# One core, attention then a SiLU block: stores moved to ScalarE's queue, early products regrouped, one bank turned, two sums of k moved

## The chip, the cores and the metric

The kernel runs on one core of one Trainium2 chip. The metric is the device time of one launch in microseconds, as the median of several runs. Engines are called PE (TensorE's matmuls), DVE (VectorE), ACT (ScalarE), POOL (GpSimd) and SP (SyncE); a "q" behind a name (SPq, ACTq) means the engine's instruction queue, from which it also issues DMAs.

## The reference, cut to what matters

```python
# q, k, v: (8 batches, 12 heads, 448 positions, 64), float32
rmsnorm = lambda x, g: x / sqrt(mean(x * x, -1) + 1e-6) * g
scores = (rmsnorm(q, g_q) @ rmsnorm(k, g_k).T) / 8
attn = softmax(scores, -1) @ v                  # (8, 12, 448, 64)
x = attn with heads side by side                # (3584, 768)
h = x @ w_in                                    # w_in (768, 2048)
out = (h * sigmoid(h)) @ w_out                  # w_out (2048, 768)
```

Everything is float32.

## The kernel before, in words

**Order of the work.** One program is written out by hand, engine by engine; each engine takes its instructions strictly in the order in which they were issued. Attention comes in 24 stretches `c`, each for four heads of one batch, so three stretches make a batch and six (`GROUP`) make two batches. A stretch is a `visit(c)` (line 1270) followed by a `between(c)` (line 1342). After stretch 5 the products with `w_in` for a finished pair of batches are laid between the stretches of the next pair; the products of the last pair, and all products with `w_out` (`quad`), come after stretch 23.

**A visit.** `scores` (L595) writes four score tiles into one of two PSUM buffers named `sc`; ACT takes their exponential (L600) and frees the buffer. There are seven such calls to a visit. `weigh` (L627) multiplies the exponentials with v into the PSUM tiles `av0` and `av1`. The visit also finishes the attention of the stretch before: for early stretches DVE copies `av` out (L1297), later ones are divided at once (`divide`, L685); `weigh(c, 0, 1)` can start only when `av` has been read.

**Beside a visit.** While stretch c runs, q and k of c+1 are normalised: `do((i, 0))` is a square on ACT (L402), `do((i, 1))` its sum on DVE (L403), a scale-and-shift (L427) and a power on POOL (L431); i = 0, 1 are the halves of q, 2, 3 those of k. For q, POOL then scales the rows (L446), and PE transposes them in `between` (L559). The flag `behind` chooses where `do((0, 1))` stands, before or after the copy of `av`. From stretch 6 on the same parts stand in the lists `further` of `between`.

**Between.** `between(c)` transposes q of c+1, calls `fill`, transposes k of c+1 (L577), adds up the exponentials (`sum_up`, L661), inverts the sums on DVE (L670, 1.5 us for each half) and spreads the reciprocals over the partitions by six SP DMAs (L677), and calls `fill` again. `fill` takes matmuls from a generator up to a due number of columns, and deals other pieces of work between them. One product is three steps, or six MATMUL instructions of 128x448.

**Products with w_in.** `Seven` makes 2x2 blocks by seven products (Strassen's way, Winograd's form). A product's PSUM bank comes from `bank`: during attention there are only the two banks `mm`, so product n+2 waits until the result of product n has been read, by ACT for the products named "1" and "5" (L781, L791), by DVE for the others (`plus`, L728), some of which POOL completes (L793, L794). After stretch 23 six more banks (`alone`) replace the attention's PSUM tiles, and every fourth product takes `mm`:

```python
        turn = turns["next"] = (turns["next"] + 1) % 4
        if ps_alone is None or turn == 0:
            return ps_mm.tile([P, BANK], F32, name="mm")[:, 0:n]
        return ps_alone.tile([P, BANK], F32, name="alone")[:, 0:n]
```

`make_ahead` computes two pairs of products of the first group in stretches 3 to 5 and stores them to DRAM (`ahead`); `fetch_ahead` brings them back. `begin` gives a generator to `fill`, with the columns due at each call. In stretches 0 to 5 `sum_up` also takes an `mm` bank.

**Stores.** When a block's two rows are complete, `activate` (line 909) takes SiLU of each on ACT (L911) and calls `save` (line 805), which stores the row to `hidden` in DRAM. The rows live in three buffers called `stage`, so a later block waits for these stores. In the last part `fetch` reads `hidden` back.

**SP's queue** carries nearly all DMAs, in order: q, k, v, the weights, the spreads, the stores of the rows and of the output. ACT's queue carries two tiny loads at the start and four small stores of the output at the very end.

**At the start** `keep_busy(4)` runs four idle 128x128 float32 matmuls, before and after a tiny transposition (L348) that needs the gains.

Of the kernel before, what the change touches and what calls it, by code (L numbers as in the profile page):

```python
# [180 lines left out]
def kernel(  # L181
# [25 lines left out]
    nc = tc.nc  # L207
# [50 lines left out]
    def load_v(c):  # L258
        main, _ = keys_of(v, c)
        dst = place["v"].rearrange("p (n j d) -> p n j d", n=4, j=z.KEYS - 1)  # L260
        nc.sync.dma_start(dst, main[:, :, 0 : z.KEYS - 1])
# [44 lines left out]
    with tc.manual_schedule(), tc.tile_pool(  # L306
        name="ps_first", bufs=1, space=bass.MemoryType.PSUM
    ) as ps_first:
        load_q(0, first_q, True, 2)
        load_k(0)  # L310
        load_q(1, second_q, True)
        load_v(0)
        for i, g in enumerate((g_q, g_k)):
            nc.scalar.dma_start(g1[:, i, :], g.rearrange("(one d) -> one d", one=1))
        load_k(1)
        load_v_rest(0)
        room.w_in.load()
        load_v_rest(1)
        nc.gpsimd.memset(minus_half, -0.5)
        make_identity(nc, ident)  # L320
        nc.scalar.activation(first, minus_half, AF.Square)


        nc.gpsimd.memset(ones[:, 0], 1.0)
        for i in range(2):
            for half in range(2):
                rows = ds(half * z.LEFT, z.LEFT)
                nc.gpsimd.memset(ones[rows, 1 + i], 1.0 if i == half else 0.0)

        wide = [g1[:, i : i + 1, :].to_broadcast([1, 2, D]) for i in range(2)]  # L330
        nc.vector.tensor_tensor(out=both, in0=wide[0], in1=wide[1], op=ALU.mult)
        nc.vector.tensor_reduce(
            out=most, in_=both[:, 0, :], axis=AX.X, op=ALU.max, apply_absolute_value=True
        )
        nc.vector.tensor_scalar(
            out=small, in0=most, scalar1=float(SCORE_MAX / D**0.5), scalar2=None, op0=ALU.is_le
        )


        idle = ps_first.tile([P, P], F32, name="idle")  # L340
        column = ps_first.tile([P, BANK], F32, name="column")[:, 0:1]

        def keep_busy(n):
            for _ in range(n):
                nc.tensor.matmul(idle, ident, ident, start=True, stop=True)

        keep_busy(4)
        nc.tensor.transpose(column, both.rearrange("p two d -> p (two d)"), ident[0:1, 0:1])  # L348
        nc.vector.tensor_scalar_mul(out=gains, in0=column, scalar1=float(D) ** -0.5)
        keep_busy(4)  # L350

        for i in range(2):
            norm.squares_q(0, first_q, first_squares[i], i)()
            norm.root(0, "q", i)
        for i in range(2):
            norm.squares_k(0, place["k0"], first_squares[i], i)()
            norm.root(0, "k", i)
            norm.scale(0, first_q, place["q0"], i, nc.vector)
# [105 lines left out]
def bounded(  # L464
# [3 lines left out]
    P, D, R, J, S = z.P, z.D, z.R, z.J, z.S  # L468
    HW, HF = z.NW // 2, z.NF // 2
# [8 lines left out]
    GROUP = z.NPAIR  # L478
# [3 lines left out]
    hidden = dram.tile([z.NF, P, z.B * S], F32, name="hidden")  # L482
# [60 lines left out]
    def x_of(c, i):  # L543
        b, cp = divmod(c, z.NPAIR // 2)
        return xT(b, 2 * cp + i)
# [205 lines left out]
    turns = dict(next=0)  # L751
# [49 lines left out]
    def staged():  # L801
        stages.append(stages.pop(0))
        return stages[-1]

    def save(f, column, t):
        nc.sync.dma_start(hidden[f, :, ds(column, t.shape[1])], t)


    AHEAD = 2
    ahead = dram.tile([AHEAD, P, 2 * S], F32, name="ahead")  # L810

    def make_ahead(group):
        for m in range(AHEAD):
            row = staged()
            yield from part_in(group, m, [row, row], True).two()
            nc.sync.dma_start(ahead[m], row)
# [384 lines left out]
    def begin(work, columns, parts):  # L1201
        finish()
        filler.update(work=work, due=0.0, share=columns / parts)
# [31 lines left out]
    def finish():  # L1235
        run(filler["work"])
# [33 lines left out]
    def visit(c):  # L1270

        beside = normalise(c + 1) if c <= GROUP else []

        def do(*which):

            if beside:
                for i, part in which:
                    beside[i][part]()

        behind = GROUP // 2 < c < GROUP  # L1280
        if c < NC:
            scores(c, 0, 0)
        do((0, 0))
        if not behind:
            do((0, 1))
        if c > 0:
            weigh(c - 1, LEFT)
            weigh(c - 1, LEFT - 1, 0)
        if c < NC:
            scores(c, 0, 1)  # L1290
        if c == 0:
            do((1, 0), (1, 1))
        if c > 0:
            weigh(c - 1, LEFT - 1, 1)
            if c - 1 < EARLY:
                for i in range(2):
                    nc.vector.tensor_copy(x_of(c - 1, i), sums[i])  # L1297
                if behind:
                    do((0, 1))
                do((1, 0), (1, 1))  # L1300
                if inverting:
                    if c > 1:
                        divide(c - 2, None)
                    run_all(inverting)
                    inverting.clear()
            else:
                divide(c - 1, sums)
                do((1, 0), (1, 1))
                if c < NC and c % GROUP == 0:
                    for i in summed_x(c):  # L1310
                        sum_x(last_two(c), i, range(3))
                if c == NC:
                    sum_x(last_two(c), 0)
                weights_in_visit(c)
            if c + 1 < NC:
                loads["vrest"](c + 1)
        if c == NC:
            return
        scores(c, 1, 0)
        scores(c, 1, 1)  # L1320
        if c < GROUP:
            do((2, 0))
        weigh(c, 0, 1)
        scores(c, 2, 0)
        if c < GROUP:
            do((3, 0))
        weigh(c, 1, 1)
        scores(c, 2, 1)
        weigh(c, 0, 0)
        run_all(add(c, 1))  # L1330
        if c < GROUP:
            do((2, 1), (3, 1))
        weigh(c, 1, 0)
        scores(c, LEFT)
        if c + 1 < NC:
            loads["v"](c + 1)

    def run_all(work):
        for piece in work:
            piece()  # L1340

    def between(c):

        def transposes_and_sums():
            summing = sum_up(c)
            if c < GROUP:
                next(summing)
            if c < NC - 1:
                transpose_k(c + 1)
            reciprocals = next(summing)  # L1350
            if GROUP // 2 <= c <= EARLY:
                divide(c - 1, None)
            return reciprocals

        if c < NC - 1:
            transpose_q(c + 1)
        if c < GROUP // 2:
            inverting.extend(transposes_and_sums())
        elif c == GROUP - 1:
            run_all(transposes_and_sums())  # L1360
        if c >= GROUP and c % GROUP == 0:
            fetched = range(AHEAD) if c == GROUP else ()
            columns = products - 2 * HW * S * len(fetched)
            work = halves_in(last_two(c), range(HF), plain_in, dict(begun), fetched)
            begin(work, columns, 2 * GROUP)
            begun.clear()
        late = add(c, LEFT - 1) + add(c, LEFT) if c >= GROUP else []
        further = [
            lambda a=a: run_all(a) for a in (normalise(c + 2) if c >= GROUP - 1 else [])
        ]  # L1370
        rest = []
        if c >= GROUP and c % GROUP == 0:
            rest = [lambda i=i: sum_x(last_two(c), i, (3,)) for i in summed_x(c)]
        fill(rest + late + weights_in(c, 0) + further[2:])
        prompt = transposes_and_sums() if GROUP // 2 <= c != GROUP - 1 else []
        if c == GROUP // 2:
            begin(make_ahead([0, 1]), AHEAD * 2 * HW * S, GROUP - 1)
        fill(weights_in(c, 1) + (further[:2] if c >= GROUP else []), prompt)
        if c % GROUP == GROUP - 1:
            finish()  # L1380
            if c == GROUP - 1:
                begun[0] = fetch_ahead([0, 1], 0)
            elif c < NC - 1:
                sum_x([c // GROUP * 2, c // GROUP * 2 + 1], 0)
        if GROUP <= c < NC - 1:

            nc.scalar.activation(first, minus_half, AF.Exp)
        if c == NC - 1:
            while rounder.load():
                pass  # L1390
# [12 lines left out]
    ps_alone = ctx.enter_context(  # L1403
        tc.tile_pool(name="ps_alone", bufs=6, space=bass.MemoryType.PSUM)
    )
    turns["next"] = 1
    group = [z.B - 2, z.B - 1]
    for i in (1, HW - 1):
        sum_x(group, i)
# [217 lines left out]
```

## Time and profile before

| | |
|---|---|
| three runs | 1351.76, 1352.02, 1356.16 us; median 1352.02 |
| the profiled run | 1354.68 us, its span 1352.8 us |
| busy, share of the span | PE 98%, DVE 68%, PEld (weight loads) 62%, ACT 38%, POOL 25% |
| stretches 0 to 5, to the first product of stretch 6 | 0 to 140 us |
| stretches 6 to 23 | 140 to 768 us |
| last pair's products with `w_in`, then those with `w_out` | 768 to 895 us, then to the end |
| `hidden` stores | 64 of 448 KB, issued by SP, median 2.7 us to landing |

Times are counted from the span's start. "Idle before" is the time in which an engine did nothing before an instruction, with what ended the wait behind the arrow; a chain of waits names, for each engine, who waited for whom and for how long in all, how often, and at most. In a row of the timeline the first number is the start, the second the length of a merged run of equal instructions.

### The profile page before, as it was taken

How to read it: one execution, taken by the hardware profiler on the slowest of the kernel's cores; microseconds unless marked ns; L12 is line 12 of the kernel's file. 1: busy time of each engine (PE TensorE's matmuls, PEld its weight loads, DVE VectorE, ACT ScalarE, POOL GpSimd, SP SyncE). 2: the span in 40 equal slices, each digit the busy share in tenths (PEclk: the TensorE clock that was granted, in tenths of full speed). 3: DMA queues.
4: the chain of work that ended last, by engine and by line, in shares of the span. 5: the costliest groups of instructions: out<-in, count | busy, mean ns of one | idle time of the engine just before them, and what ended most of it. 6: DMA issues, size and time to landing. Idle time of an engine off the chain costs nothing.

```text
span 1352.8 us, 19797 instructions
## 1 busy us (share of the span) xinstructions
PE 1323.9 (98%) x7345; PEld 837.8 (62%) x7345; DVE 921.2 (68%) x1593; ACT 517.4 (38%) x884; POOL 340.6 (25%) x241
## 2 busy tenths in 40 slices
PE   8999999999999999999999999999999999999997
PEld 4333444444444444444444455557999999999997
DVE  5887867785654444644443587679878787878785
ACT  7866565555455545454644244320000010101000
POOL 5655533343233332333221144420000000000001
PEclk9999999999999999999999999999999999999999
DMA  8554436323223223322321248521423232322311
GB/s 226 163 148 134 118 94 174 104 79 87 71 84 92 79 75 90 85 79 79 79 79 38 100 160 264 159 97 45 127 74 98 75 98 78 101 87 91 112 60 39
DMA packets 175422, 139.42 MB, mean 103 GB/s; under 512 B 104052, under 2 KB 159284, under 8 KB 175316
## 3 DMA queue, kind: packets, MB, share of 16 engines
q1 hardware_dynamic: 174640, 137.08, 34.3%
q8 instruction: 60, 0.98, 0.3%
q0 software_dynamic: 352, 0.79, 0.2%
q14 instruction: 46, 0.38, 0.1%
q10 hardware_dynamic: 324, 0.20, 0.1%
HBM read 88.47 MB, written 41.29 MB: 96 GB/s over the span
## 4 chain that ended last, share of the span: by engine, by line
PE 87%; DVE 5%; issue 3%; ACT 2%; DMA 1%; POOL 1%; SPq 0%; ACTq 0%; DVEq 0%; POOLq 0%
PE mm L773 28%; PE alone L1080 22%; PE av L627 8%; PE mm L1080 7%; PE sc L595 7%; PE alone L773 7%; PE alone L1117 2%; PE sc L559 1%; PE sc L577 1%; PE sc L661 1%; DVE work L670 1%; PE mm L1117 1%; ACT work L600 1%; PE mm L661 1%; DVE work L641 0%
## 5 line engine op out<-in xcount | busy, mean ns | idle before, releaser
L773 PE MATMUL mm<-x,W 128*128 128x448 f32 x636 | 255.4, 545 | 4.5 <-DVE stage L728 2.2
L600 ACT ACTIVATE work<-sc,rms 128x448 f32<-128x448 f32 x324 | 184.6, 633 | 91.1 <-PE sc L595 80.4
L431 POOL TENSOR_TENSOR rms<-rms,minus_half 128x14 f32<-128x14 f32 (+4 forms) x55 | 136.2, 2478 | 252.5 <-DVE rms L427 158.2
L773 PEld LDWEIGHTS mm<-x,W 128*128 128x128 f32 x636 | 118.4, 191 | 126.9 <-issue 107.3
L773 PE MATMUL mm<-sums_x,W 128*128 128x448 f32 x456 | 183.3, 542 | 1.4 <-DVE parts L728 1.1
L641 DVE TENSOR_TENSOR work<-work 128x896 f32<-128x896 f32 (+1 forms) x114 | 125.0, 1129 | 65.9 <-ACT work L600 65.4
L595 PE MATMUL sc<-work 64*64 64x448 f32 x1344 | 164.2, 547 | 1.7 <-ACT work L600 0.7
L627 PE MATMUL av<-work,rows 64*64 64x448 f32 x1296 | 152.5, 544 | 7.5 <-issue 2.6
L773 PEld LDWEIGHTS mm<-sums_x,W 128*128 128x128 f32 x456 | 85.1, 190 | 87.5 <-issue 80.6
L458 POOL DMA_DIRECT2D out_dram<-x x4 | 2.2, 565 | 442.7 <-DVE x L728 442.7
L627 PEld LDWEIGHTS av<-work,rows 64*64 64x64 f32 x1296 | 51.9, 132 | 94.6 <-issue 84.1
L595 PEld LDWEIGHTS sc<-work 64*64 64x64 f32 x1344 | 52.1, 133 | 83.7 <-issue 37.1
L1080 PE MATMUL alone<-W,rows 128*128 128x192 f32 x488 | 92.0, 326 | 0.0
L403 DVE TENSOR_REDUCE rms<-squares 112x8 f32<-112x512 f32 (+1 forms) x80 | 52.4, 655 | 55.1 <-ACT squares L402 54.3
L793 POOL TENSOR_TENSOR parts<-parts,stage 128x448 f32<-128x448 f32 x31 | 42.1, 1358 | 176.4 <-DVE parts L728 176.2
L1080 PEld LDWEIGHTS alone<-W,rows 128*128 128x128 f32 x488 | 81.4, 190 | 0.0
L1080 PE MATMUL alone<-W,work 128*128 128x192 f32 x382 | 72.2, 326 | 0.0
L911 ACT ACTIVATE stage<-stage 128x896 f32<-128x896 f32 x63 | 57.2, 945 | 26.0 <-DVE stage L728 25.4
L402 ACT ACTIVATE squares<-rows 128x512 f32<-128x512 f32 (+1 forms) x74 | 44.8, 605 | 50.6 <-DVE rms L403 49.3
L1080 PEld LDWEIGHTS alone<-W,work 128*128 128x128 f32 x382 | 63.8, 190 | 0.0
L1090 ACT COPY squares<-alone 128x192 f32<-128x192 f32 x34 | 10.8, 318 | 138.0 <-PE alone L1080 79.0
L685 DVE TENSOR_TENSOR x<-av,work 128x448 f32<-128x448 f32 x38 | 22.0, 620 | 60.9 <-PE av L627 60.5
(248 smaller groups left out, 2153.4 us busy)
## 6 DMA issues: line engine op xcount, KB each, us to landing
hidden<-stage SPq DMA_DIRECT2D x63, 448.0 KB, 2.7
work<-hidden SPq DMA_DIRECT2D x21, 1024.0 KB, 4.9
rows<-in_moe_w_out_dram SPq DMA_DIRECT2D x32, 384.0 KB, 3.5
W<-in_moe_w_in_dram SPq DMA_DIRECT2D x22, 512.0 KB, 4.8
rows<-in_k_dram SPq DMA_DIRECT2D x48, 192.0 KB, 3.1
work<-work SPq DMA_DIRECT2D x144, 56.0 KB, 1.9
rows<-in_q_dram SPq DMA_DIRECT2D x36, 224.0 KB, 3.5
x<-hidden SPq DMA_DIRECT2D x7, 1024.0 KB, 5.6
```

The costliest lines, as they stand in the source:

```text
L402: nc.scalar.activation(t, rows, AF.Square)
L403: return lambda: nc.vector.tensor_reduce(out=out, in_=t.rearrange("p (n d) -> p n d", n=n), axis=AX.X, op=ALU.add)
L431: nc.gpsimd.tensor_tensor(out=t, in0=t, in1=half, op=ALU.pow)
L595: nc.tensor.matmul(two[ds(half * D, D), h, 0:S], keys[rows, ts(half, D)], qT[rows, pair, :], start=True, stop=True,)
L600: nc.scalar.activation(eleft[:, h] if j == LEFT else weights(c, j)[:, i, h], two[:, h, 0:S], AF.Exp, scale=norm.column(c, i, h, j),)
L627: nc.tensor.matmul(sums[i][ds(h * D, D), :], v, w, start=(j == 0 and step == 1), stop=(j == LEFT - 1 and step == 1),)
L641: nc.vector.tensor_tensor(out=total, in0=total, in1=more, op=ALU.add)
L773: nc.tensor.matmul(t, self.left(name, s), self.right(name, s), start=s == ends[0], stop=s == ends[1])
L793: nc.gpsimd.tensor_tensor(out=u2, in0=u2, in1=p5, op=ALU.add)
L911: nc.scalar.activation(t, t, AF.Silu)
L1080: nc.tensor.matmul(t, x[:, i], y, start=i == ORDER[0], stop=i == ORDER[-1])
L1117: nc.tensor.matmul(o, a[:, 2 * i + m, t], right_one(name, i)[:, m], start=n == 0, stop=n == len(steps) - 1,)
```

## The change

It does five things:

- the stores of `save` are issued by ACT's queue instead of SP's;
- `begin` gives `make_ahead` its columns in 4 parts instead of 5: one whole product at each of four calls of `fill` (stretch 3's second, both of stretch 4, stretch 5's first), where before they were 3, 2, 3, 2 and 2 matmul steps;
- `turns["next"]` starts at 3 after attention, so the last group's first product takes a bank `mm`, and the following three take `alone`;
- `behind` now means stretches 1 to 3 instead of 4 and 5. In stretches 4 and 5 q's first sum moves ahead of the copy of `av`, and in stretches 0, 4 and 5 k's two sums follow their squares instead of standing at the end of the visit. In stretches 1 to 3 the order stays what it was;
- one more idle matmul at the start.

```diff
-        keep_busy(4)
+        keep_busy(5)
         nc.tensor.transpose(column, both.rearrange("p two d -> p (two d)"), ident[0:1, 0:1])
...
     def save(f, column, t):
-        nc.sync.dma_start(hidden[f, :, ds(column, t.shape[1])], t)
+        nc.scalar.dma_start(hidden[f, :, ds(column, t.shape[1])], t)
...
-        behind = GROUP // 2 < c < GROUP
+        behind = 0 < c <= GROUP // 2
         if c < NC:
             scores(c, 0, 0)
-        do((0, 0))
-        if not behind:
-            do((0, 1))
+        do((0, 0), (0, 1))
...
                     nc.vector.tensor_copy(x_of(c - 1, i), sums[i])
-                if behind:
-                    do((0, 1))
                 do((1, 0), (1, 1))
...
         if c < GROUP:
-            do((2, 0))
+            do((2, 0)) if behind else do((2, 0), (2, 1))
         weigh(c, 0, 1)
         scores(c, 2, 0)
         if c < GROUP:
-            do((3, 0))
+            do((3, 0)) if behind else do((3, 0), (3, 1))
...
-        if c < GROUP:
+        if behind:
             do((2, 1), (3, 1))
...
-            begin(make_ahead([0, 1]), AHEAD * 2 * HW * S, GROUP - 1)
+            begin(make_ahead([0, 1]), AHEAD * 2 * HW * S, AHEAD * 2)
...
-    turns["next"] = 1
+    turns["next"] = 3
```

## The prediction

> **What bounds the kernel.** First the engines' shares, then PE's waits:
>
> ```profile
> PE 1323.9 (98%) x7345; PEld 837.8 (62%) x7345; DVE 921.2 (68%) x1593; ACT 517.4 (38%) x884; POOL 340.6 (25%) x241
> ```
>
> ```profile
> PE mm L773 <- DVE stage L728: 2.4, 2, 2.2
> PE mm L773 <- DVE parts L728: 2.1, 2, 1.1
> PE alone L773 <- DVE x L685: 1.2, 1, 1.2
> PE av L627 <- DVE x L1297: 1.0, 2, 0.8
> ```
>
> PE is the bound; only its waits (some 22 us in all) can be gained, and any new one is lost in full. I then placed these waits. The longest is in stretch 4 (timeline, DVE's row, then PE's):
>
> ```profile
> 100.00 1.54 DVE L670 RECIPROCAL work<-mm 128x224 f32<-128x224 f32 x1
> 101.46 0.56 DVE L728 TENSOR_TENSOR stage<-mm,stage 128x448 f32<-128x448 f32 x1
> ```
>
> ```profile
> 102.07 3.30 PE L773 MATMUL mm<-x,W 128*128 128x448 f32 x4 [2.20 <-DVE stage L728]
> ```
>
> A product begun in one fill ends in the next, so its reading stands behind a reciprocal, and the next product has no bank. The four matmuls after it take 3.30 us, not 4 x 0.376. The stage table says why (length, PE, PEld, DVE, ACT, POOL busy, then PEclk):
>
> ```profile
> 98.40:101.70 3.30, 1.47 (x10) 0.30 (x2) 3.30 (x4) 1.07 (x2) 1.19 (x1) 1.00 0.30 65
> 101.80:105.10 3.30, 3.03 (x4) 1.17 (x4) 3.23 (x6) 0.00 (x0) 1.43 (x1) 0.50 0.99 287
> ```
>
> The clock fell to 0.50 for one stretch: 1.6 us lost.
>
> Then ACT, DVE and PE beside the saves. Stretch 11 (ACT's rows, then DVE's):
>
> ```profile
> 323.76 1.79 ACT L911 ACTIVATE stage<-stage 128x896 f32<-128x896 f32 x2
> 325.45 0.62 ACT L402 ACTIVATE squares<-rows 128x512 f32<-128x512 f32 x1
> 326.82 0.52 ACT L402 ACTIVATE squares<-rows 128x384 f32<-128x384 f32 x1 [0.75 <-DVE rms L403]
> ```
>
> ```profile
> 326.10 0.69 DVE L403 TENSOR_REDUCE rms<-squares 128x8 f32<-128x512 f32 x1 [3.36 <-ACT squares L402]
> 326.70 0.61 DVE L728 TENSOR_TENSOR stage<-mm,stage 128x448 f32<-128x448 f32 x1
> 328.05 1.55 DVE L670 RECIPROCAL work<-sc 128x224 f32<-128x224 f32 x1
> 329.52 0.56 DVE L728 TENSOR_TENSOR parts<-mm,stage 128x448 f32<-128x448 f32 x1
> ```
>
> The SiLUs end, k's squares follow with no gap, DVE idles for them, and behind its sums stand two readings of banks. The second ends at 330.08; PE takes that bank at 330.33: 0.25 us of slack. What ACT does longer before 325.45, PE pays but for 0.25.
>
> Last, what an issue on ACT's queue costs (the kernel's end):
>
> ```profile
> 1343.03 0.55 ACTq L458 DMA_DIRECT2D out_dram<-work  x1
> 1343.67 0.32 ACT L1094 COPY rows<-alone 128x192 f32<-128x192 f32 x1 [5.20 <-PE alone L1080]
> ```
>
> The copy's product ended at 1343.27; the copy before it (1338.15) began 0.08 us after its product, this one 0.40 after, 0.10 behind the issue. The issue seems to hold ACT.
>
> **The Trainium skill.** "TensorE: Matmul & The Clock Gate", section "Architectural detail", says that ACT and DVE are strict FIFO: the rows above agree. The same page, "What's actually happening", gives a free-running window of 3413 ns after whose activity the clock is set; the half-speed stretch of about 3.4 us fits. "DMA: Bandwidth & Descriptors", section "Issuing engines are not separate DMA queues", says that another issuing engine saves only sequencer time. Here ACT loses what SP saves, and SP is no bound.
>
> **The change part by part.** Per save, SP's issues (0.32 to 0.53 us) become ACT's. Four issues on ACT at the end take 0.37 to 0.55; a restart costs 0.10, and the 0.09 by which ACT's instructions now overlap is lost. Bounds: 0 (if the copy above was late for another reason), 0.46 (no restart) to 0.74; I take p = 0.65, so 1.3 a pair. Behind the pair stand squares, copies out of banks, a table load and exponentials. Of 24 pairs beside attention most are followed by over 2 us of ACT idling for PE. These are not:
> - stretch 7: DVE's reading at 190.20 waits for squares behind the SiLUs, and PE already waits there (0.62): 2p.
> - Before 326.10, 433.08, about 540 and 647 (same rows, 0.25 slack): 4 x (2p - 0.25).
> - A table load and exponentials right behind. A visit starts its first exponential normally 1.07 us after its first scores and then lasts 11.7 us. Visits 12 and 18 start at 3.20 and last 11.98 and 12.01, visit 10 3.30 and 12.11: a visit absorbs 3.20 - 1.07 - 0.28 = 1.85. Visits 13 and 19 start at 2.67, so 0.25 is left: 2 x (2p - 0.25). Visit 10: 2p. In visits 12 and 18 the SiLUs stand 1.29 us apart, which hides the first save: 2 x (p - 0.1). Visit 9 (1.82): 0.2.
>
> Together 18p - 1.7, plus 0.2: 10.2 us at 0.65, 6.6 at 0.46, 12.0 at 0.74. After 768 us eight banks rotate and PE has no wait; nothing there.
>
> SP, rid of the stores, no longer waits for SiLU (150.5 us in 50 waits) with spreads and loads behind it; no PE gap after 226 us ends on these, so 0, but for one: at 215.53 a store issued behind 1.4 MB of loads lands after 6.2 us, ACT's copy waits 4.36 us for the buffer, DVE is late and PE waits 1.14 at 225.80. In a ring of its own the store should land somewhat earlier: 0 to 1.1, taken 1.0.
>
> Stretches 3 to 6: in visit 4 the moved sum and shift (0.69 + 0.17) push the copy of `av`: PE's wait at 85.55 grows by 0.87. POOL's rows come sooner: waits of 0.11 and 0.28 go. The wait of 2.20 and the slow clock (1.6) go. Stretch 4 has one step more (0.75), stretch 5 one less, without its wait of 0.62 for ACT. Visit 5 starts 2.20 + 1.6 + 0.11 - 0.87 - 0.75 = 2.3 earlier, visit 6 2.3 + 0.28 + 0.62 + 0.75 = 3.95. But the spreads of stretch 5, issued 2.6 earlier (2.3 + 0.28), hold `divide` until about 128.65, its first half ends at 129.2, and PE, due at 132.00 - 3.95 = 128.05, waits 1.15. DVE then works back to back to 159, so 2.8 is kept, 1.2 where the clock didn't fall; bounds 0 to 4. k's sums, placed where DVE idles (2.95 us before 91.31, 3.77 before 116.04), and stretch 0's are hidden: 0.
>
> The bank: PE waits 1.24 for the last `divide`, though products 1 and 2 need only older x. `mm` was read by 763.00, so it starts at once: 1.2 (0 to 1.24).
>
> The start: matmuls run at half speed (seven transpositions 1.70 us at 6.14, 0.98 at 24.03) until 13 us. One more idle pair (0.43) fits into PE's gap of 0.62, so it delays nothing, and may bring the clock up a window earlier; the first exponential could come 1.3 us sooner. 0 to 1.3, taken 0.4.
>
> Sum against the span of 1352.8: 10.2 - (1.0 + 2.8 + 1.2 + 0.4) = +4.8. The profiled run took 1354.68, 2.7 above the median; the clock's fall (1.6) may be missing in the median run. Then +6.4: 1352.0 + 4.8 to 6.4 is 1356.8 to 1358.4. I take 1357.6.
>
> **The rivals.**
> - *The issue hardly holds ACT.* The place is the queue slot behind each SiLU, the price p; 18p - 1.7 falls below the gains of 5.4 at p = 0.39. At p near 0 the time is 1352.0 - 3.8 to 5.4: 1346.6 to 1348.2. Against it: the late copy at 1343.67; for it: one case only, and its releaser is named as PE.
> - *About even*, p near 0.4 or half the places with more slack than I read: 1349 to 1355.
> - *New slow clocks:* PE's wait of 1.63 at 85.55 lies in one window; a fall there costs 1.6, and with p = 0.74 the time is 1361 to 1363.
> - *Parts do nothing:* closing the attention's pool may hold the first product in any bank, or the early store land no sooner: 1 us each, inside the main range.
>
> **How the numbers follow.** Chances: ACT held 0.52 (own range 1355 to 1360.5), not held 0.20, about even 0.20, slow clocks 0.08. A measurement of this kernel can tell about 0.3%, 4 us, from no change: below 1348.0 is faster, above 1356.1 slower. Faster: 0.16 of the 0.20 and 0.03 of the even case, 0.19. Slower: 0.44 of 0.52, 0.02 and 0.08, 0.54. Within: 0.27. The range leaves out a tail on each side: 1347 to 1362.
>
> **What would show it.** Right: ACTq issues of 0.35 to 0.55 behind each L911; PE waits of about 1 us near 326, 433, 540, 647 on DVE L728, and longer visits 10, 12, 13, 18, 19 (12.3 to 13.4); no wait of 2.2 near 100; PE busy across 767. Wrong: the next ACT instruction starting during the issue, or those PE gaps absent.

## The result and the profile after

The changed kernel takes 1358.83 us in the median of four runs (1358.13 to 1359.25), where four runs of the kernel before took 1351.89 in the median: ratio 1.0043, 95% interval 1.0023 to 1.0064. It is slower by about 6 us: 5.8 by the ratio, which is that of the means (one of the four runs before took 1356.16), 6.9 by the medians. The forecast was 1357.6.

First the engines' busy time of the changed kernel, then its list of waits (who waits for whom: us in all, times, the longest), PE's rows alone:

```profile
PE 1322.9 (98%) x7347; PEld 833.8 (61%) x7347; DVE 920.4 (68%) x1593; ACT 522.1 (38%) x884; POOL 339.4 (25%) x241
```

```profile
PE sc L595 <- ACT work L600: 4.0, 7, 1.1
...
PE mm L773 <- ACT stage L791: 2.5, 4, 0.6
PE mm L773 <- DVE parts L728: 2.1, 6, 0.9
...
PE mm L773 <- DVE stage L728: 0.9, 5, 0.2
```

and two lines of the same list of the kernel before:

```profile
PE sc L595 <- ACT work L600: 0.7, 2, 0.6
...
PE mm L773 <- ACT stage L791: 0.6, 1, 0.6
```

PE's work is the same to 1 us; its waits are others. The wait of 2.2 for `stage` and the 1.2 for the bank at 768 are gone. In their place stand many short ones: seven for exponentials (two before), four for ACT's copy L791 (one before), eleven for DVE's readings (four before). A wait can cost more than the view prints. The view lets a matmul end 0.539 us after its start, while the next one normally starts after 0.376, and behind a wait of 0.622 the second matmul followed the first after 0.480: 0.622 + 0.163 + 0.104 = 0.89 us are lost, and stretch 16, whose only change is one such wait, is longer by just that.

Stretch 11, in the timeline of the changed kernel (first number the start, second the length). ACT's rows:

```profile
320.01 0.95 ACT L911 ACTIVATE stage<-stage 128x896 f32<-128x896 f32 x1
320.99 0.33 ACTq L806 DMA_DIRECT2D hidden<-stage  x1
321.36 0.95 ACT L911 ACTIVATE stage<-stage 128x896 f32<-128x896 f32 x1 [0.40 <-ACT stage L911]
322.34 0.35 ACTq L806 DMA_DIRECT2D hidden<-stage  x1
322.73 0.63 ACT L402 ACTIVATE squares<-rows 128x512 f32<-128x512 f32 x1 [0.43 <-ACT stage L911]
```

The store goes out 0.03 us after its SiLU's end and takes 0.33; only then does the next activation start. Two SiLUs and the step to the squares, 1.69 us in the kernel before (323.76 to 325.45), now take 2.72: a pair of stores holds ACT for 1.03 us. PE's rows of the same stretch:

```profile
324.67 2.52 PE L773 MATMUL mm<-sums_x,W 128*128 128x448 f32 x6 [0.18 <-DVE stage L728]
327.43 4.78 PE L773 MATMUL mm<-x,W 128*128 128x448 f32 x12 [0.24 <-DVE parts L728]
```

These are the two readings that stood behind k's first sum, now late. The stretch is 0.95 us longer (against the kernel with the stores on SP, told below). In visit 10 it is an exponential that comes late, and PE waits for a buffer `sc`:

```profile
269.40 0.98 PE L595 MATMUL sc<-work 64*64 64x448 f32 x8 [1.15 <-ACT work L600]
```

In stretch 4 nothing stops PE now; the stage table for two neighbouring windows of the changed kernel (columns as in the prediction; behind PEclk stand the DMA engines' busy share and GB/s) shows PE busy throughout at full clock:

```profile
94.10:97.40 3.30, 3.30 (x23) 1.38 (x26) 2.23 (x4) 1.50 (x3) 1.65 (x2) 1.00 0.56 114
97.50:100.80 3.30, 3.30 (x21) 1.32 (x14) 2.36 (x4) 2.06 (x3) 0.00 (x0) 1.00 0.78 228
```

### The profile page after: what moved, and what is told of

Its sections match the earlier page's. It is cut to its first block, busy times and chain, and to the rows that moved or that the text cites. A ratio compares the mean times of both kernels' runs of the same rounds, so it can differ in the third digit from the quotient of the medians.

```text
span 1356.3 us, 19777 instructions
## 1 busy us (share of the span) xinstructions
PE 1322.9 (98%) x7347; PEld 833.8 (61%) x7347; DVE 920.4 (68%) x1593; ACT 522.1 (38%) x884; POOL 339.4 (25%) x241
## 4 chain that ended last, share of the span: by engine, by line
PE 84%; DVE 5%; ACT 5%; issue 2%; DMA 1%; POOL 1%; ACTq 0%; SPq 0%; DVEq 0%; POOLq 0%
PE mm L773 25%; PE alone L1080 22%; PE av L627 8%; PE sc L595 7%; PE mm L1080 7%; PE alone L773 7%; PE alone L1117 2%; DVE work L670 2%; PE sc L559 1%; ACT stage L911 1%; PE sc L577 1%; ACT work L600 1%; DVE rms L403 1%; PE mm L661 1%; PE sc L661 1%
## 5 line engine op out<-in xcount | busy, mean ns | idle before, releaser
L773 PE MATMUL mm<-x,W 128*128 128x448 f32 x612 | 244.6, 544 | 4.5 <-ACT stage L791 2.5
L773 PE MATMUL mm<-sums_x,W 128*128 128x448 f32 x480 | 194.2, 543 | 1.1 <-DVE stage L728 0.9
L773 PEld LDWEIGHTS mm<-x,W 128*128 128x128 f32 x612 | 112.8, 190 | 124.2 <-issue 102.4
L773 PEld LDWEIGHTS mm<-sums_x,W 128*128 128x128 f32 x480 | 89.2, 190 | 93.3 <-issue 83.3
L1090 ACT COPY squares<-alone 128x192 f32<-128x192 f32 x33 | 10.5, 318 | 141.5 <-PE alone L1080 78.1
L670 DVE RECIPROCAL work<-sc 128x224 f32<-128x224 f32 x36 | 55.6, 1547 | 8.4 <-PE sc L661 8.2
```

The costliest lines, as they stand in the source:

```text
L670: nc.vector.reciprocal(out=r[0][:, rows], in_=t[:, rows])
L773: nc.tensor.matmul(t, self.left(name, s), self.right(name, s), start=s == ends[0], stop=s == ends[1])
```

## The experiments

The theory: each store on ACT's queue stands behind its SiLU, holds ACT until that SiLU has ended and for the issue besides, and what is queued behind it comes late; PE pays about 10 us for this in stretches 7 to 20, and the other parts bring 4 to 5 us. The rivals: the other parts cost the time, or a ring of its own (another engine's queue of DMAs) for the stores matters more than ACT. The ratios below are to runs of the kernel before on the same chip (medians there 1352.6 to 1353.0).

| kernel | median us | ratio, 95% interval |
|---|---|---|
| all but the stores | 1348.49 | 0.9968 (0.9959 to 0.9977) |
| only the stores | 1363.33 | 1.0074 (1.0060 to 1.0088) |
| after, second store of a pair on ACT | 1351.88 | 0.9993 (0.9985 to 1.0002) |
| after, ACT's queue only after stretch 23 | 1348.82 | 0.9974 (0.9963 to 0.9985) |
| only the products ahead in 4 parts | 1350.61 | 0.9986 (0.9979 to 0.9993) |
| only the sums moved | 1352.34 | 0.9995 (0.9986 to 1.0003) |
| only the idle matmul and the bank | 1352.12 | 0.9990 (0.9981 to 0.9998) |
| only the products ahead and the bank | 1349.56 | 0.9977 (0.9967 to 0.9986) |
| all but the stores, spreads of stretch 5 shared with POOL | 1351.67 | 0.9990 (0.9983 to 0.9996) |
| the same, shared with ACT | 1351.53 | 0.9991 (0.9983 to 0.9999) |
| after, the pairs of stores later | 1355.79 | 1.0025 (1.0016 to 1.0035) |

### Where the stores are issued

**All but the stores.** In the kernel after:

```diff
-        nc.scalar.dma_start(hidden[f, :, ds(column, t.shape[1])], t)
+        nc.sync.dma_start(hidden[f, :, ds(column, t.shape[1])], t)
```

> The kernel after with its stores of hidden back on SP's queue; all else as in after. Theory (the stores hold ACT about 0.5 us each, and PE pays about 10 us of it in stretches 7 to 20): the 10 us go, and at most 1 us of gain goes with them (the early store in a ring of its own, stretch 8): 1348.8 to 1349.8 us, ratio to before 0.997 to 0.999; the PE waits of about 0.9 us near 324, 434, 543, 653 (behind DVE's readings) and near 405, 514, 624 (behind ACT L791) are gone, visits 10, 12, 13, 18, 19 last 12.1, 12.0, 11.7, 12.0, 11.7 us again. Rival A (the other four parts cost the time, the stores are hidden): stays at 1358.8. Rival B (the own ring for the stores is itself worth several us, offset by its cost): over 1352.

Measured: 4.3 us faster than before (3.1 to 5.5), at 1348.49 just under the theory's range; both rivals fall. The waits of PE for exponentials, for L791 and for DVE's readings go back to what they were, and visit 23 starts 10.5 us sooner than in the kernel after. No kernel that was run was faster. But the "1 us that goes with the stores" didn't go: with the stores in SP's ring PE had no wait near 222 us (0.19 in the kernel after).

**Only the stores**, in the kernel before the same line the other way round:

> The kernel before with its stores of hidden on ACT's queue; nothing else of the change. Theory: plus 10 us in stretches 7 to 20, minus 1 us where the store of 215 us lands sooner in a ring of its own: 1352.0 + 9.0 = 1361 us (1360 to 1362). The starts of visits 3 to 7 stay within 0.5 us of before; visit 9 starts about 1 us earlier against visit 8 than in before; a pair of stores delays the first exponential of visit 10 by 1.03 us. Rival A (stores hidden, loss from the re-ordering): 1352. Rival B (stores and the earlier start of stretch 6 collide, so the loss needs both): 1353 to 1357.

Measured: 10.0 us slower (8.1 to 11.9). Rivals A and B fall. The median of 1363.33 is over the expected 1360 to 1362: the kernel before took 1353.0 here, not 1352.0, and one point of the expectation was wrong, since the gain at stretch 8 didn't come. The copy L791 that waits for the first store to land, in the kernel with only the stores on ACT, and in the kernel with all on SP:

```profile
221.09 0.53 ACT L791 COPY stage<-mm 128x448 f32<-128x448 f32 x1 [2.56 <-DMA hidden<-stage]
```

```profile
216.30 0.53 ACT L791 COPY stage<-mm 128x448 f32<-128x448 f32 x1 [3.21 <-DMA hidden<-stage]
```

In the first the store went out on ACT at 215.53 and landed after 5.5 us, and PE waited 1.15; in the second it went out on SP at 211.69 and landed after 4.5, and PE waited for nothing. So a ring of its own didn't make this store land in time.

**Half of them.** In the kernel after:

```diff
-        nc.scalar.dma_start(hidden[f, :, ds(column, t.shape[1])], t)
+        queue = nc.scalar if f % 2 else nc.sync
+        queue.dma_start(hidden[f, :, ds(column, t.shape[1])], t)
```

> The kernel after with only the second store of each pair on ACT's queue, the first on SP's. Theory (loss grows with the time that ACT is held, one price of 0.51 us a pair instead of 1.03): stretch 7 0.3, the readings near 324, 434, 543, 653 0.26 each, visits 13 and 19 0.26 each, visit 10 0.3, visits 12 and 18 0.37 each (their second store is the one not hidden), 405, 514, 624 about 0.4 each: some 4.1 us over the kernel with all stores on SP, so about 1353 (1352 to 1354.5). Rival (the loss comes from having a second ring at all, or from one delayed instruction whatever the length): as after, 1358, or as with all on SP, 1349.

Measured: 1351.88, just under the expected range, 3.4 us over the kernel with all stores on SP, and 3.7 in the two spans (1349.5 and 1345.8). The loss grows with the time that ACT is held, and both cases of the rival fall. The three places near 405 us and on cost nothing here, though, where 0.4 each was expected; the section on the prediction comes to these.

**After stretch 23 only.** In the kernel after, `queue = nc.sync if ps_alone is None else nc.scalar`:

> The kernel after with the stores of hidden on SP's queue until stretch 23 ends, and on ACT's from then on (12 blocks of the last group). Theory (with eight banks rotating PE waits for no reading there): within 0.3 us of the kernel with all stores on SP, 1348.8 to 1349.8. Rival (the stores cost after stretch 23 too, 24 x 0.5 us of ACT): up to 1361 less the loss before it, that is 1352 to 1358.

Measured: 1348.82, the same as with all on SP within the noise. The 16 stores after stretch 23 (the expectation counted 24), where eight banks rotate, cost nothing on ACT that can be measured.

### The start, stretch 4 and the store of stretch 8: the kernel before once more

> The kernel before, unchanged, profiled once more. Theory (the late start and the half-speed clock of stretch 4 in the first profile of before were chance, since the kernel with only the stores moved showed neither and still has before's start and its wait of 2.2 us): visit 1 starts at 25.3 to 25.5 us instead of 26.58, the granted clock near 100 us stays at 0.99 behind the wait of 2.2 us, and the span is 2 to 3 us shorter, about 1350. Rival (both belong to the order of before): visit 1 at 26.6, half clock near 103 us, span 1352.8. The wait of 1.14 at 225.80 should come again if it belongs to before's order; if it hangs on how the loads happen to land, it is between 0 and 1.2.

Half of it failed. The span was 1352.0 and visit 1 started at 26.37: the late start came again. So did the half clock, from 102.5 to 105.9 us. PE's wait in stretch 8 was 0.39 instead of 1.14, on the same program: the store of 215 us, issued by SP both times, landed after 5.4 us instead of 6.2. So the wait hangs on how the transfers happen to land. Taking all profiles together: with four idle matmuls visit 1 started at 26.58, 26.37, 27.50, 25.43, 25.33 and 25.25 us, with five at 25.1 to 25.4 in six kernels and at 26.07 and 25.84 in two, in which the clock had come up and fell again at 10 us. Both occur with both; whether the fifth matmul makes the early start likelier, these few profiles don't settle.

### The other parts one by one

**Only the products ahead**: in the kernel before, `GROUP - 1` becomes `AHEAD * 2` in `begin(make_ahead(...))`.

> The kernel before with only the columns of the products made ahead given out in 4 parts, one whole product to a call. Theory (this is what brings the gain in stretches 3 to 6, by taking away the waits of 2.2 and 0.62 us): from the start of visit 3 to that of visit 7 about 100.7 us, 2.4 less than the 103.1 that the kernels with before's order took; ratio to before 0.998 (1349.5 on a base of 1352). Rival (the gain needs the new order of DVE too, since the division of stretch 6 waits for spreads and gives all back): 103 us and no change in the time.

Measured: 1.9 us faster (0.9 to 2.8). From visit 3 to visit 7 it took 100.33 us, as expected, where the kernel before took 103.16 and 103.14 in its two profiles, the kernel with only the stores moved 103.07 and that with only the start and the bank changed 103.83 (its clock was at 0.50 from 68.3 to 71.8 us). The rival falls.

**Only the sums moved**: the diff's hunks with `behind`.

> The kernel before with only the new meaning of the flag behind (q's first sum and k's sums moved in stretches 0, 4 and 5). Theory (it moves DVE's work within its idle time, and costs the copy of av in stretches 4 and 5 what it gives to POOL's rows): visit 3 to visit 7 within 0.5 us of 103.1, time within 0.1% of before. Rival (it is this that brings the gain): 100.5 us, ratio 0.998.

Measured: 0.7 us faster, not told from nothing (1.9 faster to 0.4 slower). In the trace it took 101.55 us from visit 3 to 7, which neither expected: PE's wait in stretch 4 fell from 2.20 to 1.24. It adds nothing to the products ahead, which bring 100.33 without it and 100.26 with it: both end at the same later wait, that for the division of stretch 6 (1.24 and 1.65 us).

**Only the start and the bank**: `keep_busy(5)` and `turns["next"] = 3` in the kernel before.

> The kernel before with only the fifth idle matmul at the start and the first bank of the last group turned. Theory: PE's gap of 1.24 at 767 goes and the end comes 1.2 us sooner; the start of visit 1 is the same as in other profiles of kernels with four idle matmuls (25.3 to 25.5), so the ratio is 0.9991 (0.9985 to 0.9997). Rival A (closing the attention's pool holds the product anyway): ratio 1.000. Rival B (the fifth matmul brings the clock up sooner and is worth 1.3 us more): 0.998.

Measured: 1.35 us faster (0.3 to 2.6). The gap of 1.24 is gone. From the start of visit 23 to PE's last matmul the kernels with the bank turned take 615.40 us, those without 616.71, so the gap cost 1.31. Rival A falls, and rival B's ratio lies at the edge of the interval; the start is as told above.

**Products ahead and bank together**:

> The kernel before with two parts of the change alone: the columns of the products made ahead in 4 parts, and the first bank of the last group turned. Theory (these two are all that gains): visit 3 to visit 7 100.3 us as with the first part alone, no gap of 1.24 at the last group's start, so 2.8 + 1.2 us less: ratio 0.9970, as of the kernel with only the stores put back (0.9968). Rival (the new order of the sums or the fifth idle matmul is worth a us as well): 0.998.

Measured: 3.1 us faster (1.9 to 4.5), 100.21 us from visit 3 to 7, no gap at the bank. Its interval overlaps that of the kernel with all parts but the stores, so these two parts bring the most of it; that the other two bring nothing isn't shown.

### The wait that gives back, and the order on ACT

**Three of six spreads on another queue.** In the kernel after with the stores on SP:

```diff
-                    nc.sync.dma_start(mine[i][m, h], mine[0][i, h])
+                    queue = nc.gpsimd if c == GROUP - 1 and h else nc.sync
+                    queue.dma_start(mine[i][m, h], mine[0][i, h])
```

> The kernel after with its stores of hidden on SP again, and of the six spreads of stretch 5 three issued by POOL's queue instead of SP's. With all six on SP they go out one after the other from 120.60 to 125.44, divide starts at 126.88, and PE waits 1.65 at 125.91. Theory (what is won in stretches 4 and 5 is given back at this wait, so shortening the row of issues keeps it): the last spread lands about 1.5 us sooner, the wait falls below 0.5, visit 7 starts 1.0 to 1.6 us sooner than the 159.02 of the kernel with the stores on SP: ratio to before 0.996. Rival (DVE's work from 127 to 159 is the next bound, or POOL's issues are slower than SP's): the start of visit 7 moves by less than 0.5 us.

and the same with `nc.scalar`:

> As the run with three spreads on POOL's queue, but these three on ACT's. Theory: at 120.6 ACT has just gone idle (0.92 us before the first exponential of visit 6), so two issues of 0.33 to 0.55 us fit in about there and the third delays an exponential by 0.5 us at most; PE's wait for divide falls from 1.65 to below 0.8: visit 7 starts 0.5 to 1.5 us sooner than 159.02. Rival (ACT is held behind the wait of the third spread for the first two to land, with exponentials queued behind it): PE waits 1 to 3 us for exponentials in visit 6, and visit 7 starts later than 159.0.

Both are slower than without the edit, by about 3 us, and visit 7 started later, at 163.19 and 162.27. Both theories fall. On POOL the last spread was issued at 125.96, landed 3.9 us later (1.9 on SP), and PE waited 3.87. On ACT the spreads landed early, but the rival came in full. ACT's rows, then PE's, then the stage table:

```profile
120.62 3.48 ACTq L678 DMA_DIRECT2D work<-work  x3
124.15 0.65 ACT L90 ACTIVATE W<-W 128x512 int32<-128x512 uint32 x1 [7.20 <-DMA work<-work]
```

```profile
128.47 1.02 PE L595 MATMUL sc<-work 64*64 64x448 f32 x4 [4.18 <-ACT work L600]
```

```profile
124.00:127.00 3.00, 0.29 (x4) 0.00 (x0) 1.03 (x2) 2.85 (x6) 0.00 (x0) 1.00 0.81 219
127.00:130.50 3.50, 2.03 (x12) 0.61 (x16) 3.27 (x8) 3.50 (x8) 3.03 (x2) 0.53 0.54 166
130.50:134.00 3.50, 3.50 (x24) 1.17 (x20) 3.40 (x8) 2.21 (x5) 3.25 (x2) 0.50 0.00 0
```

ACT's third issue went out at 123.58, after the first four spreads had landed (the last of them at 123.51), and until then ACT's queue stood still, with all the exponentials behind it. PE waited 4.18, and its clock was at 0.50 from 127.2 to 134.0. Whether a shorter row of spreads would keep the time won in stretches 4 and 5 was therefore not seen; it stays open.

**The pairs of stores later, still on ACT.** In the kernel after `activate` only lists the rows, and they are stored one product later:

```diff
             nc.scalar.activation(t, t, AF.Silu)
-            save(f, b * S, t)
+            unsaved.append((f, b * S, t))
...
+                    if count > 2 * HW:
+                        save_all()
                     if count > HW:
                         activate(owed)
```

Some rows are overwritten by the next block before they are stored, so a part of `hidden` holds later rows; the number of DMAs and instructions is that of after.

> The kernel after with the stores of hidden still on ACT's queue, but each pair issued at the start of the next product but one after the one at which its SiLUs stand, so behind the squares, copies or exponentials that in after stood behind the stores. Theory (the loss is the delay of what stands right behind the SiLUs, not the use of ACT's queue): first exponentials of visits 13 and 19 again at 2.67, of visit 10 at about 3.3; no PE wait near 324, 434, 543, 653 nor near 405, 514, 624: 1349 to 1352. Rival A (holding ACT costs wherever it stands): within 2 us of after, 1357 to 1359. Rival B (rows are freed a product or a whole visit later, so ACT's copies or DVE's sums wait for their landing): new PE waits of 1 us and more, 1355 or over.

Measured: 3.4 us slower than before, 2.4 less than after by the ratios. 1355.79 is outside the ranges of the theory and of rival A; it is in that of rival B, but no new wait of 1 us or more is there. ACT's rows in stretch 11 show the theory's part:

```profile
318.65 1.79 ACT L916 ACTIVATE stage<-stage 128x896 f32<-128x896 f32 x2
319.63 0.33 ACTq L806 DMA_DIRECT2D hidden<-stage  x1
320.34 0.62 ACT L402 ACTIVATE squares<-rows 128x512 f32<-128x512 f32 x1
320.47 0.33 ACTq L806 DMA_DIRECT2D hidden<-stage  x1
```

Here the queue holds both SiLUs, the squares, then both stores. The first store goes out while the second SiLU runs, and the squares begin without a gap: here an issue cost ACT nothing by itself; what it holds is what stands behind it in the queue. So only the activations among themselves kept the program's order: the store stands behind the squares in it, and went out 0.72 us before they started. The Trainium skill says why, in "Perfetto Trace Analysis": in "DVE / Act Engine Instruction" the sequencer pushes an instruction into a wait queue and goes on, in "DMA Instruction — HWDGE (DVE, Sync)" the sequencer itself waits for a DMA's semaphores. These rows agree: in the kernel after, behind none of the 64 stores did ACT start anything before the issue was over, and in this one an issue ran beside an activation. Where the order was SiLU, SiLU, store, store, squares (stretch 13), the pair cost 0.51 instead of 1.03.

By the starts of the visits the kernel loses 7.6 us against the one with the stores on SP. But the view of waits has a longer line for ACT's copies, which rival B had with another cause:

```profile
PE mm L773 <- ACT stage L791: 5.0, 8, 0.6
```

Before there was one such wait. Seven new ones of 0.62 us at 0.89 each are 6.2, so of the 7.5 us that ACT's lateness cost in the kernel after (next section) 1.4 are left. The cause of the new waits isn't a store that lands late; it is told in the next section.

## Why the prediction was right, step by step

**The price p.** Measured 1.03 us a pair, p = 0.51, inside the bounds of 0.46 to 0.74, below the 0.65 taken (at these two bounds the prediction's formula gives 6.8 and 11.8 us, not the 6.6 and 12.0 written there). The issue behind a SiLU took 0.33, not the 0.37 to 0.55 of the kernel's end, with 0.03 before and 0.04 behind it, and the lost overlap was 0.09 as assumed. The half dose agrees: 3.2 us of 7.3 in the places that aren't those near 405, 514 and 624 or stretch 8.

**The places.** The difference between after and the kernel with the stores on SP, from the start of one visit to the next, against the prediction's terms at 0.65:

| place | predicted us | measured us |
|---|---|---|
| stretch 7 | 1.3 | 0.5 |
| readings near 324, 434, 543, 653 | 4.2 | 3.8 |
| visits 13, 19 | 2.1 | 1.6 |
| visit 10 | 1.3 | 0.7 |
| visits 12, 18 | 1.1 | 0.7 |
| visit 9, stretch 8 | 0.2 | 0.2 |
| near 405, 514, 624 | 0 | 2.7 |
| sum | 10.2 | 10.2 |

That the sum is right is luck: two errors cancel, p too high by a quarter, and three places not seen. With p at 0.51 the prediction's terms make 7.7; without the three places 7.5 was measured. At stretch 7 the prediction said that DVE's reading makes PE wait, "and PE already waits there (0.62)". That wait is for ACT's copy and is still 0.62 in the kernel after; the late readings stop PE only behind it, for 0.16 at 191.29 and 0.37 at 193.93.

**What was not seen: which bank a product gets.** Stretch 13 of the changed kernel, DVE's row, ACT's and PE's:

```profile
404.56 0.61 DVE L728 TENSOR_TENSOR parts<-mm,stage 128x448 f32<-128x448 f32 x1
```

```profile
405.51 0.53 ACT L791 COPY stage<-mm 128x448 f32<-128x448 f32 x1 [1.59 <-PE mm L773]
```

```profile
406.10 1.77 PE L773 MATMUL mm<-x,W 128*128 128x448 f32 x4 [0.62 <-ACT stage L791]
```

DVE had read product "6" by 405.17, before product "5" ended at 405.47. Had product "7" taken that bank, PE wouldn't have stopped. It waits for ACT's copy of "5", which starts only when "5" has ended. In the instructions of the compiled program the first matmul of this product waits for DVE's semaphore in the kernel before, and for ACT's in the kernel after: it was given the other bank. So the rule that product n+2 takes the bank of product n isn't kept everywhere. The banks in the built programs say the same: among the tiles given out in `mm`, one has the bank of the tile just before it at three places in the kernel with all stores on SP, at the same three with one store of a pair on ACT, at six in the kernel after, and at ten where the pairs come later; in the kernel before at four, with only the stores moved at seven. The same wait on ACT stands at stretches 13, 16 and 19 in the kernels after and with only the stores on ACT, and at seven stretches where the pairs come later; with one store of a pair on ACT, and with all on SP, it is a wait for DVE, and PE goes on:

```profile
399.76 4.30 PE L773 MATMUL mm<-sums_x,W 128*128 128x448 f32 x11
403.90 1.67 PE L773 MATMUL mm<-x,W 128*128 128x448 f32 x4
```

That is the kernel with one store of a pair on ACT, at the same place: no wait. So 2.7 of the 10.2 us come from another bank in the program, not from ACT being late on the chip. Why the build gives out another bank when the stores move stays open.

**Stretches 3 to 6.** Kept: 2.8 predicted, 2.76 measured (103.16 to 100.40). Counted from visit 3, visit 5 came 2.6 earlier and visit 6 4.75 (2.3 and 3.95 predicted), and the wait for the division, predicted at 1.15, gave more back:

```profile
127.90 1.12 PE L627 MATMUL av<-work,rows 64*64 64x448 f32 x6 [1.62 <-DVE x L685]
```

But "1.2 where the clock didn't fall" failed: with before's order it took 103.07 in a profile without the slow clock and 103.16 and 103.14 in those with it. What the slow clock costs, the wait for the division gives back, since PE then comes to it later: it waited 1.00 for it in the profile without the slow clock and not at all in the kernel before. So the term of 1.6 for a median run without the fall was none.

**The early store.** 1.0 was put on a ring of its own. In the kernel after the wait is down from 1.14 to 0.19, which looks like the forecast come true. But the kernel before, profiled again, waited 0.39, and a kernel with the stores in a ring of their own waited 1.15. The step is wrong; what was read was how the transfers landed in one execution.

**The bank at 768.** 1.2 predicted, 1.31 measured.

**The start.** 0.4 taken; 1.27 between the two profiles at visit 1. By the profiles of the other kernels much of it is chance, and what the fifth matmul brings isn't shown.

**The sum.** Measured alone, the parts are 10.0 for the stores, and 1.9, 0.7 and 1.35 gained by the others: +6.0 us. The kernel with all of them took 5.8 more than before (0.43%; 3.1 to 8.7). They add up as far as the noise lets one see. The forecast's +5.6 had the right mechanism for 7.5 us of the loss; the other 2.7 made up for a price that was too high. On the side of the gains 3.8 to 5.4 was forecast and 4.3 measured with all four parts together, though the early store and the term for the clock weren't real. So the direction was earned, and that the forecast came within 1.2 us was luck.

## What to carry to other kernels

In these runs a DMA behind the instruction whose result it stores made its queue wait until that instruction had ended; on an engine that computes, put it behind the instructions that others wait for, or on a queue that computes nothing. Before reading a wait for a bank as lateness, look which bank it is: here a product that got the bank written last waited for a whole reading, however early the other one was free. And take two profiles of the same program before explaining a wait on a DMA or a clock that fell once.

## What the runs showed of the hardware

- A store behind its SiLU held ACT 0.51 us, 0.33 of it the issue; a store queued behind a second SiLU and the squares went out beside that SiLU and held nothing.
- An issue that waits for other DMAs holds everything behind it: 3.48 us on ACT for three spreads of 0.5 to 0.8 us each.
- In the same stretch the spreads issued by POOL landed after 2.2 to 3.9 us, those by SP after 1.9 to 2.1.
- With PE's waits of 3.87 and 4.18 us the clock fell to 0.50 for 6.8 us, from 1.1 and 1.3 us before the wait was over. Of seven waits between 1.9 and 2.3 us in these profiles three were followed by 3.4 us of slow clock, of the waits of 1.0 to 1.7 us none.
- A printed wait of 0.62 us between matmuls of 128x448 lost 0.89 us; one of 1.24 us behind matmuls of 64x448 lost 1.31.
